# An S4D layer and a mixture of experts on one core: decay powers in pairs, the last block transposed in SBUF, a new order for the front

## The chip, the cores and the metric

The kernel runs on one core of one Trainium2 chip. The metric is device time in microseconds (us) of one execution. Three executions of the kernel before took 728.3 to 729.1 us, with a median of 728.49.

## What is computed

One sequence of 2048 tokens with 512 channels passes through two residual layers.

```python
def A(u):                                  # S4D: a long convolution per channel
    A_ = -exp(log_A_real) + 1j * A_imag    # (512, 128), dt = exp(log_dt)
    C  = (C_real + 1j * C_imag) * dt
    K  = 2 * einsum("dn,dnl->dl", C, exp(A_ * dt * pos)).real    # 512 kernels of length 2048
    return causal_convolution(u, K) + u * D_skip

def B(x):                                  # mixture of 8 experts, one for each token
    gates = softmax(x @ wg)                # wg: 512 x 8
    h = gelu(einsum("nd,edf->nef", x, w1)) # w1: 8 x 512 x 1792
    y = einsum("nef,efd->ned", h, w2)      # w2: 8 x 1792 x 512
    return y of the token's best expert    # its weight, normalised over one choice, is 1

h   = u + A(layernorm(u))
out = h + B(layernorm(h))
```

## The kernel before

**How the order is set.** The kernel is written as some two thousand tasks. `at(engine, cost, function, arguments, r=reads, w=writes)` records one with what it reads and writes, and the table `ORD` gives each its place in the program by name and ordinal; nothing is planned from the costs while it is built. Tasks that can run on two engines carry "AV", and `ON` says for each whether it runs on ScalarE (ACT) or VectorE (DVE). The table `FILL` says after which tasks TensorE (PE) runs how many filler matmuls on zeros (L952 in the profile), keyed by a task's name and ordinal. Each engine takes its own instructions strictly in this order. Transfers are issued by SyncE's queue (SP), and those whose rows are looked up by GpSimd (POOL).

**The front, up to about 363 us.** The 512 channels are four blocks of 128. For each block, `tables` makes powers of the decay and of the rotation and multiplies them out to the convolution kernel:
- `t_e` (L612): exp(l * alp) for l = 0..63, one ACTIVATE of 128x128 for each power; `t_ep` (L572) six more for the steps of 32; `t_r6`, `t_f6` (L579, L584) round six multiples of the angle phi and subtract.
- `t_wi`, `t_wr` (L661, L663, L668) on DVE multiply powers and angles for a quarter of the block; `t_kg` (L675) is PE's sum over the 128 states, 64 small matmuls into one PSUM bank, which the trace counts as 128; `t_kt` (L679) copies the bank to SBUF and `t_d` (L683) adds D_skip to its first column.

`conv` then runs on blocks, with eight pieces (rc) each: `c_load` and `c_s2` (L544) bring the kernel into the form of short matrices, `c_z` (L735) multiplies by them on DVE, `c_ia` (L742, L743) is 16 matmuls back, and `c_ys` (L748) copies their bank to SBUF. The result has time and channel in the wrong places, so `c_yst` (L751) stores each piece to `yd_scratch` in DRAM and `c_y1` (L774) loads four quarters (q) of the block back with the axes exchanged. `c_ib` (L779) transforms each quarter (two matmuls, which the trace counts as four), `c_add` (L782) adds the residual x, and the quarter goes on to routing: `r_s4` (row statistics, L994), `r_tr` and `r_ev` (transpose by PE and copy, L999, L1003), `r_lg` (logits, L1011), and `r_hd`, the store of its rows to `hd_scratch`.

**Between the layers.** `r_st` (L990) takes statistics of the first two blocks' columns, loaded again by `r_ld`; `r_ag` (L1040) joins them; `r_sd` and `r_rs` give 1/std; `r_le` copies logits, `r_lt` transposes them, `r_a` (L1079 to L1083) picks the expert. `r_vs` (L1103) stores mean, 1/std and token number of each row in 16 bytes behind the row's 512 columns. Counts and prefix sums give each expert its list of rows (`r_B`, `r_t0`, `r_i0`, L1187).

**The experts, from about 363 us.** For each expert, `m_ga` (L1292) gathers its rows from `hd_scratch` by POOL, `m_ln` normalises (L1334), and the two matrix products run in three passes, with each operand split in a high and a low part (L1380 on ACT, L1384 on DVE; L1393 to L1395 and L1416 to L1418 or L1425 to L1427 on PE). `m_ot` (L1442) scales and adds the residual, and `m_sc` (L1285) scatters rows to the output.

## Time and profile before

| what | value |
|---|---|
| median of three executions | 728.49 us |
| the profiled execution, its own time | 730.45 us |
| span of that execution in the trace | 728.6 us |
| mean granted clock of PE | 0.968 of full speed |
| last instruction of the tables (`t_wr` of block 3) ends | 297.9 us |
| last `c_ys` (block 3) starts | 333.41 us |
| first gather of rows starts | 363.62 us |
| last scatter starts | 722.11 us |

The trace covers one execution. Its span begins at the first and ends at the last instruction, and the execution's own time is 1.85 us longer. In the lines below, "L661" is a line of the program, "out<-in" names the tiles, "x32" counts instructions, and after the bar stand busy time in us and the mean of one in ns.

### The profile page before, as it was taken

To read this page: it belongs to the slowest core of one execution; us is meant where nothing else is said; L and a number is where in the kernel's file an instruction comes from. 1 tells how busy PE (TensorE), PEld (TensorE's weight loads), DVE (VectorE), ACT (ScalarE), POOL (GpSimd) and SP (SyncE) were. 2 spreads that over 40 slices of the span, in tenths; PEclk is the share of its full clock that TensorE was granted. 3 is DMA by queue.
4 is the path that set the end of the run, shared out by engine and by line. 5 is a ranking of instruction groups with operands and counts; after the bars stand their busy time and mean duration, and the time that the engine had idled before them with its cause. 6 is when DMAs were issued, how large, how long until landed. Compare 5 with 4: busy or idle time off the path is not lost.

```text
span 728.6 us, 19922 instructions
## 1 busy us (share of the span) xinstructions
PE 657.8 (90%) x8184; PEld 577.3 (79%) x8184; DVE 565.4 (78%) x1063; ACT 455.8 (63%) x907; POOL 73.1 (10%) x65
## 2 busy tenths in 40 slices
PE   3688999988989998798779999999999999999995
PEld 2446898778777886585369999999999989898884
DVE  6999998899999998575768975666766777666752
ACT  6899999959965976111435545555555556566651
POOL 0000000000000000000015131040210302132201
PEclk9689999999999999999769999999999999999998
DMA  9994134657575696898757566456565667676620
GB/s 188 174 233 60 62 119 175 237 214 212 155 229 176 188 279 219 238 298 231 178 198 207 157 203 187 147 190 197 173 207 169 204 203 236 196 234 197 198 90 26
DMA packets 139256, 136.38 MB, mean 187 GB/s; under 512 B 42172, under 2 KB 108352, under 8 KB 138907
## 3 DMA queue, kind: packets, MB, share of 16 engines
q1 hardware_dynamic: 135674, 126.48, 60.2%
q0 software_dynamic: 3488, 8.60, 3.4%
q8 instruction: 65, 1.06, 0.6%
q14 instruction: 29, 0.23, 0.1%
HBM read 109.83 MB, written 29.52 MB: 191 GB/s over the span
## 4 chain that ended last, share of the span: by engine, by line
PE 46%; issue 18%; DVE 16%; DMA 10%; ACT 4%; SPq 2%; POOL 2%; POOLq 1%; DVEq 0%; ACTq 0%
DMA y<-yd_scratch 5%; PE ps_s L1393 4%; PE ps_s L1394 4%; PE ps_s L1395 4%; PE ps_kk L544 3%; PE pk L675 3%; PE ps_ga L742 3%; PE ps_pl L952 3%; PE ps_ga L743 3%; DMA yd_scratch<-ys 2%; PE ps_kk L1425 2%; SPq L389 2%; PE ps_s L779 2%; PE ps_kk L1427 2%; PE ps_kk L1426 2%
## 5 line engine op out<-in xcount | busy, mean ns | idle before, releaser
L1384 DVE TENSOR_TENSOR l<-r,h 128x1024 fp32r<-128x1024 f32 x112 | 136.5, 1223 | 53.0 <-ACT h L1380 50.3
L1380 ACT CAST h<-r 128x1024 fp32r<-128x1024 f32 x112 | 117.6, 1050 | 80.7 <-PE ps_s L1395 41.4
L1393 PE MATMUL ps_s<-xh,h 128*128 128x288 f32 (+5 forms) x448 | 129.8, 290 | 0.0
L1395 PE MATMUL ps_s<-xl,h 128*128 128x288 f32 (+5 forms) x448 | 128.1, 286 | 0.0
L1394 PE MATMUL ps_s<-xh,l 128*128 128x288 f32 (+5 forms) x448 | 127.9, 286 | 0.0
L1393 PEld LDWEIGHTS ps_s<-xh,h 128*128 128x128 f32 x448 | 85.5, 191 | 3.1 <-issue 0.5
L1394 PEld LDWEIGHTS ps_s<-xh,l 128*128 128x128 f32 x448 | 85.4, 191 | 2.5 <-issue 0.5
L1395 PEld LDWEIGHTS ps_s<-xl,h 128*128 128x128 f32 x448 | 85.3, 190 | 0.0
L1398 ACT ACTIVATE g<-ps_s 128x288 f32<-128x288 f32 (+5 forms) x112 | 43.3, 387 | 65.4 <-PE ps_s L1395 50.3
L1405 DVE TENSOR_TENSOR gl<-g,gh 128x288 fp32r<-128x288 f32 (+5 forms) x112 | 46.6, 426 | 20.3 <-ACT gh L1401 18.0
L952 PE MATMUL ps_pl<-ident 128*128 128x512 f32 (+1 forms) x156 | 53.9, 492 | 0.0
L612 ACT ACTIVATE e<-alp 128x128 f32<-128x128 f32 x256 | 53.2, 309 | 0.0
L742 PE MATMUL ps_ga<-u,mi 128*128 128x128 f32 x256 | 50.9, 280 | 2.4 <-issue 2.4
L743 PE MATMUL ps_ga<-u,mi 128*128 128x128 f32 x256 | 49.9, 276 | 2.5 <-issue 2.5
L1285 POOL DMA_INDIRECT out_dram<-ot,si x20 | 24.4, 1218 | 222.8 <-DVE ot L1442 219.4
L952 PEld LDWEIGHTS ps_pl<-ident 128*128 128x128 f32 x156 | 28.1, 216 | 21.2 <-issue 20.3
L735 DVE TENSOR_TENSOR u<-ps_kk,u 128x1024 f32<-128x1024 f32 x32 | 38.5, 1217 | 7.7 <-PE ps_kk L544 7.7
L742 PEld LDWEIGHTS ps_ga<-u,mi 128*128 128x128 f32 x256 | 38.8, 191 | 6.6 <-issue 5.4
L743 PEld LDWEIGHTS ps_ga<-u,mi 128*128 128x128 f32 x256 | 38.9, 192 | 2.9 <-issue 2.9
L675 PE MATMUL pk<-e,vr 128*32 128x64 f32 x1024 | 36.2, 230 | 3.4 <-issue 2.0
L675 PEld LDWEIGHTS pk<-e,vr 128*32 128x32 f32 x1024 | 33.5, 144 | 5.3 <-issue 3.5
L675 PE MATMUL pk<-wi,vi 128*32 128x64 f32 x1024 | 36.1, 228 | 1.4 <-issue 0.8
(288 smaller groups left out, 1582.4 us busy)
## 6 DMA issues: line engine op xcount, KB each, us to landing
r<-in_B_w_dram SPq DMA_DIRECT2D x112, 512.0 KB
u<-ud_scratch SPq DMA_DIRECT2D x32, 512.0 KB
ud_scratch<-xn SPq DMA_DIRECT2D x16, 512.0 KB
yd_scratch<-ys SPq DMA_DIRECT2D x32, 256.0 KB
y<-yd_scratch SPq DMA_DIRECT2D x16, 512.0 KB
xu<-in_A_u_dram SPq DMA_DIRECT2D x16, 256.0 KB
xd_scratch<-in_A_u_dram SPq DMA_DIRECT2D x8, 512.0 KB
xr<-xd_scratch SPq DMA_DIRECT2D x6, 512.0 KB
```

The source lines that it names most:

```text
L612: A.activation(tb[blk, "e"][:, l // 2, :, l % 2], par(alp, blk), AF.Exp, scale=float(l))
L675: T.matmul(pk[32 * g:32 * g + 32, 64 * j:64 * j + 64], v[:, :, 8 * g + j], w[:, :, 8 * g + j, :], start=n == 0, stop=n == 1, skip_group_ch ...
L742: T.matmul(pa[:, c], mi[:, 4 * rc + rr, 64:192], z[:, 0, c], start=True, stop=False)
L743: T.matmul(pa[:, c], mi[:, 4 * rc + rr, 0:128], z[:, 1, c], start=False, stop=True)
L952: T.matmul(p[:, 0:128 * k], w, _view(ident, [[0, k], [1, 128]]), start=first, stop=True, skip_group_check=True)
L1380: A.copy(tile_(("h" + n, e, f), list(r.shape), F32R, pool="wp", name="h" + n, bufs=2), r)
L1384: V.tensor_tensor(tile_(("l" + n, e, f), list(r.shape), F32R, pool="wp", name="l" + n, bufs=2), r, t_["h" + n, e, f].bitcast(F32), op=OP.s ...
L1393: T.matmul(o[:, 0:CAPS[e]], a, xh, start=c == 0, stop=False)
L1394: T.matmul(o[:, 0:CAPS[e]], b, xh, start=False, stop=False)
L1395: T.matmul(o[:, 0:CAPS[e]], a, xl, start=False, stop=c == 3)
L1398: A.activation(tile_(("g", e, f), [128, CAP], name="g", bufs=2)[:, 0:CAPS[e]], t_["pf", e, f][:, 0:CAPS[e]], AF.Gelu_apprx_tanh)
L1405: V.tensor_tensor(tile_(("gl", e, f), [128, CAP], F32R, name="gl", bufs=3)[:, 0:n], t_["g", e, f][:, 0:n], t_["gh", e, f][:, 0:n].bitcast( ...
```

## The change

1. **Decay powers in pairs.** alp and phi get a second copy beside them that holds twice the value (`p_tw`, two DVE instructions). One ACTIVATE over both makes the powers l and 2l of 128x2x128 elements. `t_e` is now 42 ACTIVATEs for each block, 21 pairs and 21 single ones; `t_ep` is three, `t_r6` and `t_f6` four each. Power 0 is a memset on GpSimd (`t_e0`, `t_e1`).
2. **D_skip by PE.** `t_d` is gone; a matmul of the identity with `dpad` opens the bank of `t_kg`.
3. **Block 3 without the trip to DRAM.** All 32 rows of block 3 stay in `ys3`. Four VectorE transposes by 32x32 blocks (`c_yt`) exchange the axes into `yt3`, and eight pairs of matmuls (`c_ic`) over half the columns each take the place of the four `c_ib`.
4. **Statistics with the last rows.** The last 128 columns lie in `hx` with mean, 1/std and token number behind them, so that the store of block 3's rows (`r_hd`, now issued by ACT's queue) carries all; `r_vs` is gone. `r_ld` and `r_st` work in eight halves, `r_rs` in four.
5. **End of the last expert.** The last six matmuls of each of its two chunks stand together by chunk.
6. **Order.** `ORD` has new places for the whole front and `ON` new engines for some copies; `FILL` is unchanged. Two of block 2's four `c_y1` are issued by ACT, and two use the ring of the u1 tiles.

```diff
     'p_pol': [15],
...
-    'c_ys': 'AVAAAAVAVAAAAVVAAAAAAAAAVVVAAAAA',
+    'c_ys': 'VAAVAAVAAAAAAAAAAAAAAAAAVAAAVVAA',
...
+    def p_tw(k):
+        t = (alp2, phi2)[k]
+        V.tensor_scalar(t[:, 1, :], t[:, 0, :], 2.0, None, op0=OP.mult)
...
+    def pair(t, blk, two):
+        return t[:, 0:1 + two, 128 * blk:128 * blk + 128]
...
-        for k in range(6):
-            A.activation(ep[:, k, :], par(alp, blk), AF.Exp, scale=float(32 << k if k else 0))
+        for k, n, two in ((1, 64, 1), (3, 256, 1), (5, 1024, 0)):
+            A.activation(ep[:, k:k + 1 + two, :], pair(alp2, blk, two), AF.Exp, scale=float(n))
...
-        for l in range(l0, l0 + n):
-            A.activation(tb[blk, "e"][:, l // 2, :, l % 2], par(alp, blk), AF.Exp, scale=float(l))
+    HEAD = [l for l in range(1, 64) if (l & -l) in (1, 4, 16)]
+    POWERS = [l for l in HEAD if l < 32] + [l for l in HEAD if l > 32]
+
+    def t_e0(blk):
+        nc.gpsimd.memset(mk(blk, "e", [128, 32, 128, 2])[:, 0, :, 0], 1.0)
+
+    def t_e(blk, i):
+        for l in POWERS[3 * i:3 * i + 3]:
+            a, b = (256 * (k // 2) + k % 2 for k in (l, 2 * l))
+            two = l < 32
+            A.activation(_view(tb[blk, "e"], [[b - a, 1 + two], [2, 128]], a), pair(alp2, blk, two), AF.Exp, scale=float(l))
...
+        T.matmul(_view(pk, [[64, 8]]), ident, dpad[:, 32 * blk + 8 * jc:32 * blk + 8 * jc + 8], start=True, stop=False, skip_group_check=True)
...
-    def t_d(blk, jc):
-        k0 = tb[blk, ("kt", jc)][:, :, 0]
-        V.tensor_tensor(k0, k0, dpad[:, 32 * blk + 8 * jc:32 * blk + 8 * jc + 8], op=OP.add)
...
+    def c_yt(j):
+        if ("yt", j // 2) not in cv:
+            cv["yt", j // 2] = env["wp"].tile([128, 32, 64], F32, name="yt3", tag="w2", bufs=2)
+        V.transpose(_view(cv["yt", j // 2], [[1, 32], [64, 32]], 32 * (j % 2)), _view(env["ys3"], [[1, 32], [128, 32]], 32 * j))
...
+        t = cv["y1", blk, q] = utile(False) if blk == 2 and q % 2 else mp.tile([128, 2, 512], F32, name="y1")
+        (nc.scalar if blk == 2 and q in (0, 3) else nc.sync).dma_start(t, _dram(yd, [[32 * 128, 128], [16 * 128, 2], [1, 512]], (blk * 32 * 128 + 4 * q) * 128))
...
+    def c_ic(c, q):
+        if ("po", 3, q) not in cv:
+            cv["po", 3, q] = psp.tile([128, 512], F32, name="ps_" + ("s1", "kk")[q // 2], tag=("s1", "kk")[q // 2], bufs=2)
+        for h in range(2):
+            T.matmul(_view(cv["po", 3, q][64 * h:64 * h + 64], [[128, 4], [1, 64]], 64 * c), ibc[:, 64:128],
+                     cv["yt", c][:, 16 * h + 4 * q:16 * h + 4 * q + 4, :], start=True, stop=True)
...
+        env["hx"] = hp.tile([128, 16, 132], F32, name="hx")
...
-        nc.sync.dma_start(_dram(hd, [[16 * HW, 128], [HW, 4], [1, 128]], 4 * b4 * HW + 128 * blk), hs[blk, b4])
+        last = blk == 3
+        (nc.scalar if last else nc.sync).dma_start(_dram(hd, [[16 * HW, 128], [HW, 4], [1, 128 + 4 * last]], 4 * b4 * HW + 128 * blk),
+                                                   env["hx"][:, 4 * b4:4 * b4 + 4, :] if last else hs[blk, b4])
...
-    def r_vs():
-        nc.sync.dma_start(_dram(hd, [[16 * HW, 128], [HW, 16], [1, 4]], 512), t_["val"])
...
+    def ends(e, f):
+        return e == E - 1 and f > 11 and by_token(e)
...
-            for k in chunks(e):
+            for f, k in [(n, f - 12) for n in (12, 13)] if ends(e, f) else [(f, k) for k in chunks(e)]:
```

What the new order does shows best at two places. The first is PE's program just ahead of and behind the last `c_ia` of block 3 (L742, L743 before; L759, L760 now). In the kernel before, the last two of these 16 matmuls are followed by block 2's first `c_ib` (L779), fillers, routing transposes and the other three:

```order
L742 MATMUL ps_ga<-u_4274,mi 128x128
L743 MATMUL ps_ga<-u_4274,mi 128x128
L779 MATMUL ps_s_4509<-y_4355,ibc 64x512 x2
L952 MATMUL ps_pl<-ident,zero 128x128 x3
L999 MATMUL ps_ga<-ident,xr 128x128 x8
L1011 MATMUL ps_pl<-ys,wgp 32x128 x4
L999 MATMUL ps_ga<-ident,xr 128x128 x4
L1011 MATMUL ps_pl<-ys,wgp 32x128 x8
L779 MATMUL ps_s_4563<-y_4515,ibc 64x512 x2
```

In the changed kernel two `c_ib` of block 2 (L794; one reads a y tile, one a u1 tile) stand ahead of the last `c_s2` (L550, four of its matmuls) and the last `c_ia`:

```order
L759 MATMUL ps_ga<-u_4224,mi 128x128
L760 MATMUL ps_ga<-u_4224,mi 128x128
L794 MATMUL ps_s_4353<-y_4341,ibc 64x512 x2
L794 MATMUL ps_s_4366<-u_4363,ibc 64x512 x2
L550 MATMUL ps_kk<-ks,m_84 128x128 x4
L759 MATMUL ps_ga<-u_4261,mi 128x128
L760 MATMUL ps_ga<-u_4261,mi 128x128
```

So the two transforms moved from behind block 3's last back transform to ahead of it. The second place is DVE's program at the end of the front, where "xr" and "h" are the residual tiles of blocks 2 and 3, and "st" the statistics. Before, each addition waits for a quarter's transform:

```order
L782 TENSOR_TENSOR xr<-xr,ps_s_4509 128x512
L994 BN_STATS st<-xr 128x6 x4
L1003 COPY ys<-ps_ga 128x512 x2
L782 TENSOR_TENSOR xr<-xr,ps_s_4563 128x512
L994 BN_STATS st<-xr 128x6 x4
L782 TENSOR_TENSOR h_4265<-h_4265,ps_s_4580 128x512
L994 BN_STATS st<-h_4265 128x6 x4
L782 TENSOR_TENSOR h_4265<-h_4265,ps_s_4589 128x512
L1040 BN_AGGR r_val<-st 128x2 x4
```

Now the four transposes (L769) stand between block 2's last addition and block 3's, whose residual tile is "hx":

```order
L804 TENSOR_TENSOR xr<-xr,ps_s_4366 128x512
L1022 BN_STATS st<-xr 128x6 x8
L769 STREAM_TRANSPOSE yt_4439<-ys_4013 128x32x32 x2
L769 STREAM_TRANSPOSE yt_4451<-ys_4013 128x32x32 x2
L1018 BN_STATS st<-hr 128x6 x2
L1088 CAST r_cb<-r_rt 128x264
L804 TENSOR_TENSOR hx<-hx,ps_s_4457 128x4x128
L804 TENSOR_TENSOR hx<-hx,ps_s_4462 128x4x128
L1022 BN_STATS st<-hx 128x6 x4
L804 TENSOR_TENSOR hx<-hx,ps_kk 128x4x128
```

Two of block 2's additions and their statistics moved to ahead of the last `c_ys`, and the transposes stand where DVE waited for loads.

More of the change, by code (lines that the diff above doesn't have):

```diff
@@ new lines @@
+    'p_ev': [18, 20, 79],
+    'p_tw': [19, 23],
+    'p_at': [21],
+    't_e0': [22, 201, 391, 559],
+    't_e1': [24, 152, 383, 508],
+    't_r': [25, 188, 372, 542],
+    't_r6': [28, 85, 287, 555],
+    't_e': [29, 67, 36, 33, 59, 46, 64, 51, 57, 40, 69, 42, 45, 32, 228, 214, 244, 224, 241, 254, 248, 249, 218, 203, 262, 211, 231, 206,
+        414, 422, 410, 432, 399, 398, 400, 417, 402, 424, 421, 401, 413, 420, 611, 580, 607, 565, 617, 590, 570, 566, 595, 561, 585, 574,
+        594, 583],
@@ new lines @@
+    'p_th': [30],
+    'l_s1': [31],
+    'u_stats': [60, 34, 49, 80],
+    't_f': [35, 41, 48, 52, 55, 58, 196, 215, 220, 225, 243, 256, 376, 378, 389, 405, 418, 427, 546, 549, 552, 560, 576, 581],
+    'x_cp': [43, 50, 235, 158, 111, 198, 68, 39],
+    't_ep': [44, 191, 384, 544],
+    't_f6': [47, 129, 331, 569],
+    't_vf': [54, 56, 61, 62, 73, 177, 179, 187, 189, 195, 374, 377, 385, 388, 437, 597, 598, 601, 606, 620],
+    'u_mean': [63, 83],
+    'u_dev': [65, 89],
+    't_tb': [66, 115, 131, 154, 268, 308, 326, 358, 433, 461, 486, 524, 614, 653, 679, 708],
@@ L347, in s4d @@
     cp = st.enter_context(tc.tile_pool(name="s4c", bufs=1))
-    phi = cp.tile([128, 512], F32, name="phi")
-    alp = cp.tile([128, 512], F32, name="alp")
     amp = cp.tile([128, 512], F32, name="amp")
@@ L368, in s4d @@
     ta = tsa.enter_context(tc.tile_pool(name="s4tab2", bufs=1, side="right", reuse_waits="tile"))
+    phi2, alp2 = (ta.tile([128, 2, 512], F32, name=n) for n in ("phi", "alp"))
+    phi, alp = phi2[:, 0, :], alp2[:, 0, :]
     at = plan.add
-    ldt = cp.tile([128, 4], F32, name="ldt")
-    dt4 = cp.tile([128, 4, 4], F32, name="dt4")
-    dtw = cp.tile([128, 4, 4], F32, name="dtw")
+    ldt = fp.tile([128, 4], F32, name="ldt")
+    dt4 = fp.tile([128, 4, 4], F32, name="dt4")
+    dtw = fp.tile([128, 4, 4], F32, name="dtw")
     stt6 = fp.tile([128, 64, 6], F32, name="stt6")
@@ L804, in conv @@
             at("AV", EV, c_ys, blk, rc, r=["pa" + j] + ["h3/0/o"] * last, w=[y])
-            at("S", 0.87, c_yst, blk, rc, r=[y], w=[f"yd{n}/{rc}"])
-        ys = [f"{('yh', 'yk')[q // 2] if last else 'y1'}/{4 * blk + q}" for q in range(4)]
+            if not last:
+                at("S", 0.87, c_yst, blk, rc, r=[y], w=[f"yd{n}/{rc}"])
+        ys = ["yt" if last else f"{'ub' if blk == 2 and q % 2 else 'y1'}/{4 * blk + q}" for q in range(4)]
         for q in range(4):
@@ L816, in conv @@
             if last:
[L817 to L818 removed]
+                j = f"{('po', 'pv')[q // 2]}/{12 + q}"
+                for c in range(2):
+                    at("T", 0.55, c_ic, c, q, r=[f"yt/{c}", "ibc/0"], w=[f"{j}/{c}"])
+                at("V", 0.66, c_add, 3, q, r=[j, "hq/0", "hq/1"], w=[f"h3/0/{q}"])
                 route(blk, q, [f"h3/0/{q}"])
@@ L1314, in m_wu @@
     def m_wu():
-        V.memset(sm("wui", [PR, 1], I32), 0)
-        gather(sm("wur", [PR, 128]), t_["wui"], cst["id"])
+        V.memset(eid[:, 0:1], 0)
+        gather(sm("wur", [PR, 128]), eid[0:PR, 0:1], cst["id"])
     def m_ga(e, k):
```

421 lines of the change are left out of this document (204 added, 217 removed), and 91 rows, old and new, of tables (ORD, RINGS).

## The prediction

> **What bounds the kernel now.** I read the page first, then busy time by stage, then the chain of work that ended last.
>
> ```profile
> span 728.6 us, 19922 instructions
> PE 657.8 (90%) x8184; PEld 577.3 (79%) x8184; DVE 565.4 (78%) x1063; ACT 455.8 (63%) x907; POOL 73.1 (10%) x65
> ```
>
> PE is busy 90% of the span, but that is an average, and in the front it includes fillers that serve no result. The windows by stage say more. Their columns are the stretch, its length, busy us of PE, weight loads, DVE, ACT and POOL, the granted PE clock, the DMA share and GB/s.
>
> ```profile
> 57.00:298.00 241.00, 218.47 (x4937) 187.79 (x4935) 226.80 (x300) 197.37 (x422) 0.00 (x0) 1.00 0.56 178
> 65.00:328.00 263.00, 236.25 (x5109) 204.87 (x5110) 237.85 (x331) 194.24 (x421) 1.13 (x1) 1.00 0.62 194
> 328.00:363.00 35.00, 26.74 (x207) 15.57 (x206) 22.56 (x83) 10.60 (x19) 0.00 (x0) 0.88 0.76 205
> ```
>
> From 57 to 298 us DVE is busy 226.8 of 241 us: it paces the tables. From 328 to 363 us no engine is full, so the chain there is latency. What DVE waits for in the first stretch, in its view of waits (total us, times, longest):
>
> ```profile
> DVE wi L661 <- ACT ks L530: 2.0, 1, 2.0
> ...
> DVE wi L661 <- ACT s L579: 0.8, 1, 0.8
> ```
>
> Only 2.8 us of its 14.2 us idle is put down to ACT. The chain (start, us, what) then gives the hand-over to the experts:
>
> ```profile
> 298.81 1.08 PE ps_s L779 x4
> 299.89 2.26 PE pk L675 x107
> ...
> 316.25 0.89 PE ps_kk L544 x8
> 317.14 0.22 PE ps_ga L742 x2
> ...
> 333.41 0.59 ACT ys L748
> 334.02 2.49 DMA yd_scratch<-ys
> ...
> 337.22 8.30 DMA y<-yd_scratch
> ...
> 357.20 6.41 DMA r<-in_B_w_dram
> 363.62 5.75 DMA rows<-hd_scratch,r_gi
> ```
>
> After the last `c_ys` at 333.41, which I call E, 12.1 us pass in a store and a load until block 3's y is there (337.22 + 8.30), and 30.2 until the first gather at 363.62. From there the experts run, PE bound: nothing in them changes but the last 12 matmuls and some early placements, so what the gather gains, the end gains.
>
> **The tables.** Their last DVE instruction ends at 297.9; the groups of DVE (count, then busy us and mean ns) and of ACT:
>
> ```profile
> L530 DVE COPY ks<-ps_s 128x512 f32<-128x512 f32 x14 | 9.4, 685 | 3.9 <-PE ps_s L525 3.9
> L514 DVE TENSOR_SCALAR xn<-xu,mr 128x128 f32<-128x128 f32 x28 | 7.6, 430 | 0.0
> L584 DVE SCALAR_TENSOR_TENSOR s<-phi,s 128x128 f32<-128x128 f32 x24 | 5.2, 281 | 0.0
> L683 DVE TENSOR_TENSOR kt<-kt,dpad 128x8 f32<-128x8 f32 x16 | 2.7, 168 | 0.0
> L663 DVE TENSOR_TENSOR wi<-e,rf 128x1024 f32<-128x1024 f32 x16 | 19.5, 1219 | 0.0
> L445 DVE RECIPROCAL cw<-cw 128x512 f32<-128x512 f32 x1 | 3.4, 3353 | 0.0
> ...
> L612 ACT ACTIVATE e<-alp 128x128 f32<-128x128 f32 x256 | 53.2, 309 | 0.0
> L468 ACT COPY phi<-ps_s 128x512 f32<-128x512 f32 x1 | 0.6, 568 | 0.0
> ...
> 274.92 0.16 DVE L683 TENSOR_TENSOR kt<-kt,dpad 128x8 f32<-128x8 f32 x1
> 274.99 0.28 DVE L634 TENSOR_TENSOR vi<-amp,ep 128x128 f32<-128x128 f32 x1
> ...
> 296.67 1.22 DVE L668 TENSOR_TENSOR e<-e,af 128x1024 f32<-128x1024 f32 x1
> ```
>
> On DVE up to that instruction: six fewer copies of a PSUM bank (counted from `ON` and the order) at 0.67 (9.4/14), -4.0. Fifteen `t_d`: the next instruction starts 0.07 behind one, so I take 0.08 each, -1.2; the bound by the group's 0.168 is -2.5. `t_f6` goes from six to four each block; a pair should lie between 0.22 (5.2/24) and 0.69, I take 0.36, so 6 x 0.22 - 2 x 0.22 - 2 x 0.36 = 0.15 a block, -0.6. Four more `u_norm` instructions at 0.27, +1.1. `p_tw` is two of 512 elements, between 0.3 and 0.69 each, +0.8. The sum is **-3.9**.
>
> On ACT, 64 exponentials of 0.21 a block (53.2/256) become 21 of 256 elements and 21 of 128. The 512-element copy takes 0.57, so between the two 256 elements cost about 0.33, and a block saves 13.3 - 21 x 0.33 - 21 x 0.21 = 2.0, or 8 us in all; `t_ep` and `t_r6` save some 2.6 more, by the same prices, and six copies come in at 0.57, +3.4, less four norms of 0.2 or more. ACT is thus relieved of about 8 us, but it is not what DVE waits for: I price it at **0**, with -2.8 as the bound of the two rows above, and what a better order might do to the rest of DVE's idle time as a rival. The first exponential of a block now waits for a POOL memset, which waits for PE to be done with the block before. POOL is idle there (0.00 in the first window), and ACT has PSUM copies of 0.57 beside it; if that cover fails, four memsets of 128 elements a row that are as slow per element as L445, +3.4 at most. The identity matmul of `t_kg` is 16 small ones among 2048, **0**.
>
> **From the last table to E.** After it `t_kg` (2.26) and then block 3's pieces follow on PE with little room: 298 to 333 is a row of matmuls. Now two `c_ib` of block 2 stand ahead of the last two `c_ia`. Each is 1.08 (row 298.81), so +2.2. These two wait for their loads of y; PE cannot pass them, and the last `c_s2`, `c_ia` and so everything behind wait for it. Both loads are issued by ACT, in its order behind a `c_ys`, and one needs the y tile that the `c_ib` before it leaves. A load like it took between 5.0 us in block 2 and 8.3 in block 3:
>
> ```profile
> 293.65 5.02 DMA y<-yd_scratch
> ```
>
> In between PE has two `c_s2` (rows of eight matmuls in the chain, 0.89) and two `c_ia` (16 matmuls of 0.11, 1.8), 5.4 us. The wait is 0 for a load of 5.02 and 2.9 for one of 8.30, and could occur at both. I take +1.0, near the load of its own block, with 0 to 5.8 as ends. From the tables to E: **+3.2**, and E itself moves by -3.9 + 3.2 = -0.7.
>
> **From E to the gather.** DVE in the kernel before (start, us, in the bracket the idle time ahead):
>
> ```profile
> 350.09 0.51 DVE L1040 BATCH_NORM_AGGREGATE r_val<-st 128x2 f32<-128x18 f32 x4
> 350.52 0.81 DVE L994 BATCH_NORM_STATS2 st<-h 128x6 f32<-128x128 f32 x4
> 351.24 0.67 DVE L782 TENSOR_TENSOR h<-h,ps_s 128x512 f32<-128x512 f32 x1
> 351.83 0.51 DVE L1040 BATCH_NORM_AGGREGATE r_val<-st 128x2 f32<-128x18 f32 x4
> 354.77 0.29 DVE L1017 COPY r_ls<-ps_pl 128x128 f32<-128x128 f32 x1 [1.08 <-PE ps_pl L1011]
> 362.31 0.15 DVE L1187 TENSOR_REDUCE r_gi<-ps_kg 128x3 int32<-128x6 f32 x1
> ```
>
> Now `c_ys` takes 0.6 behind E, DVE has block 2's last addition and statistics to finish (0.35 more), and the four transposes start at E + 0.95. **No transpose is in the trace.** Each handles 1024 elements a row, as L663 does in 1.22 (1.13 from start to start). Ends: 0.7, were it twice as fast as that row per element less its fixed part, and 6.7, were it as slow per element as L445 (3.35 for 512). I take 1.13, the row with its size: E + 5.45. [...]
>
> Behind them DVE's work stands nearly without a gap. From the last addition's start to `r_gi`'s end it took 362.46 - 351.24 = 11.2 us, of which 1.1 idle (row 354.77) and 0.5 `r_ls` copies, which go to ACT, fall away: 9.6. New in front or in between are three additions (0.59 each from start to start, 1.8), three groups of statistics (0.72, 2.2), two of aggregates (0.43, 0.9), eight `r_st` of 0.18 with the cast and PE's step to the first addition (2.4): 7.3. So `r_gi` ends at E + 5.45 + 16.9 = E + 22.35, and the gather starts at E + 22.6 if it waits for nothing else. It waits too for the last store of rows. That is now issued by ACT when DVE has the last 1/std, about 5 us ahead of `r_gi`; the store in the chain took 2.49, so it lands at about E + 21, 1.6 us to spare. In the kernel before, `r_gi` ended at 362.46 and the gather started at 363.62, so something else, by the order the 16-byte store `r_vs`, held it; that is gone. From E to the gather 30.2 become 22.8: **-7.4**.
>
> **The end.** PE's matmuls stand 0.23 apart:
>
> ```profile
> 717.14 0.39 PE L1416 MATMUL ps_kk<-h,gh 128*128 128x512 f32 x1
> 717.37 0.39 PE L1417 MATMUL ps_kk<-l,gh 128*128 128x512 f32 x1
> ...
> 719.42 1.13 DVE L1442 SCALAR_TENSOR_TENSOR ot<-ps_kk,cwt,rows 128x128 f32<-128x128 f32 x4 [2.23 <-PE ps_kk L1418]
> ...
> 722.11 0.96 POOL L1285 DMA_INDIRECT out_dram<-ot,si  x1 [0.30 <-issue]
> ```
>
> The first chunk is done three matmuls earlier, so its scaling and scatter come 0.7 earlier; the second scatter then waits for the second chunk's scaling (done at 721.58) and not for POOL: **-0.6**.
>
> **Sum.** -3.9 + 3.2 - 7.4 - 0.6 = -8.7. The profiled execution of 730.45 (span 728.6 and 1.85 around it) becomes 721.75; it lies 1.96 above the median, so the forecast is 728.49 - 8.7 = **719.8**.
>
> **Rivals.**
> - *Loads hold PE ahead of E.* Both `c_ib` wait 2.9 us: +4.8 on the forecast, 724.6. For it speaks the one load of 8.30, against it those of block 2. Chance 0.17.
> - *DVE's idle time shrinks with ACT's load.* If half the 14.2 us goes: 712.7. Against it speaks that only 2.8 is put down to ACT; for it, that the rest is waits on PE banks which ACT's copies also free. 0.14.
> - *Slower: the fillers no longer fall in PE's gaps.* `FILL` is keyed by task and ordinal, and those tasks have moved. From 65 to 328 us the granted clock is 1.00. Where PE idled it fell:
>
> ```profile
> 365.70:369.10 3.40, 0.01 (x1) 0.00 (x0) 0.00 (x0) 1.04 (x1) 1.03 (x2) 0.91 1.02 394
> 369.10:372.50 3.40, 2.03 (x9) 1.66 (x10) 2.37 (x5) 0.43 (x1) 0.00 (x0) 0.50 0.03 12
> ```
>
> A gap of 3.4 us put the next stretch to half clock. Each us of PE work at half clock takes twice as long; with PE on the path, 17.4 us of span at half clock eat the gain of 8.7, and 30 us (a fall in each of the four blocks, each over twice the 3.4 of the second row) give 719.8 + 15 = 734.8. [...] Chance 0.12.
> - *The change doesn't do what it says:* a transpose costs 3.35, L445's time, not 1.13: +8.9, 728.7, no change. 0.07.
>
> **How the numbers follow.** The forecast (716.5 to 723 by the ends of its small terms) has 0.50. A measurement of this kernel can tell about 0.2% from no change, that is 727.0 to 729.9. Faster: 0.50 + 0.17 + 0.14, less a margin for sums of mishaps, 0.80; same 0.08; slower 0.12. The range of 712.0 to 728.5 takes in all but the slower rival, half the last one, and the far end of the second.
>
> **What would show it.** Right: `t_wr` of block 3 ends near 294, no ACT wait on DVE, the transposes take 1.1 each, gather 22 to 23 us behind the last `c_ys`, the clock at 1.00 up to 328. Wrong: PE idle on y ahead of the last `c_ia` for over 3 us; transposes over 2 us; a clock below 1.00 there; the gather released by a store.

## The result, and the profile after

The changed kernel takes 738.59 us (median of four executions, 736.65 to 740.25), the kernel before, beside it, 728.39 (726.67 to 729.10). The ratio is 1.0143, with a 95% interval of 1.0105 to 1.0180: the change makes the kernel 1.4% slower. The forecast of 719.8 and its range were missed on the other side. The profiled execution of the changed kernel took 736.95 us. In what follows medians are over all executions of a run, and ratios leave out single executions that were slow (the slowest: one of 2233 us in `f1_half_fill` and one of 1876 us in `f4_half_weights_loads`).

The page, as before (span, then busy us, share and count by engine):

```profile
span 735.0 us, 19910 instructions
PE 657.4 (89%) x8244; PEld 583.2 (79%) x8244; DVE 567.5 (77%) x1042; ACT 457.1 (62%) x806; POOL 76.1 (10%) x73
```

The sums hardly differ, so the time went into waits and into where the work stands. The span is therefore cut at the same four events in both traces (te: end of the last `t_wr`; E: end of the last `c_ia`; start of the first gather; end of the span):

| stretch | before, us | after, us | forecast | measured |
|---|---|---|---|---|
| start to te | 297.9 | 300.8 | -3.9 | +2.9 |
| te to E | 35.4 | 41.5 | +3.2 | +6.1 |
| E to gather | 30.3 | 32.2 | -7.4 | +1.9 |
| gather to end | 365.0 | 360.5 | -0.6 | -4.5 |
| span | 728.6 | 735.0 | -8.7 | +6.4 |

Of the last -4.5, 2.0 only give back the row above: the rows, gathered later, landed in 3.67 us (5.75 before), so that the first expert matmul starts 40.7 us behind E before and 40.6 after. The other 2.5 are more than the forecast's 0.6; a second profile of the unchanged kernel (`b0_before_again`, below) already differs from the first by 1.2 there, and the rest was not taken apart. The windows of the changed kernel (columns as in the prediction), for the whole tables and then for the prediction's three stretches:

```profile
0.00:300.80 300.80, 253.05 (x5066) 211.24 (x5066) 273.41 (x447) 243.99 (x448) 1.84 (x12) 0.97 0.67 176
57.00:298.00 241.00, 219.38 (x4949) 191.37 (x4948) 221.43 (x280) 196.22 (x340) 1.29 (x6) 0.99 0.56 171
65.00:328.00 263.00, 237.47 (x5174) 209.42 (x5168) 227.68 (x284) 191.97 (x337) 2.42 (x7) 0.97 0.59 181
328.00:363.00 35.00, 28.42 (x262) 19.89 (x260) 30.84 (x91) 11.66 (x22) 0.00 (x0) 0.98 0.59 155
```

The same sum over the tables of the kernel before:

```profile
0.00:297.90 297.90, 254.60 (x5036) 208.38 (x5036) 276.66 (x471) 245.80 (x556) 0.20 (x4) 0.97 0.67 182
```

DVE's work fell by 3.25 us, close to the forecast, and yet te is not earlier: DVE idles 27.4 us in place of 21.2. In the second profile of the unchanged kernel te is 300.6 and DVE idles 24.1 us. So the +2.9 in the table is not told from spread; what both profiles show is that the 3 us of work that DVE was spared became idle time. Its waits up to te, the largest of the changed kernel (total us, times, longest):

```profile
DVE xn L560 <- PE ps_kk L550: 5.7, 5, 3.9
DVE u L752 <- PE ps_kk L550: 3.8, 3, 2.1
DVE vi L653 <- PE pk L695: 3.3, 1, 3.3
```

All name PE. In the kernel before the largest two were these, 3.1 and 2.6:

```profile
DVE u L735 <- PE ps_kk L544: 3.1, 4, 1.8
DVE xn L554 <- PE ps_kk L544: 2.6, 5, 1.0
```

The chain that ended last, behind te (start, us, what), shows the rest of the story:

```profile
297.76 2.21 PE ps_pl L980 x18
...
303.93 3.44 issue
307.37 1.98 PE ps_s L531 x45
309.34 1.58 PE ps_pl L980 x6
...
314.04 1.57 PE ps_pl L980 x6
...
330.36 6.10 DMA u<-yd_scratch
...
342.37 0.59 ACT ys L764
...
344.88 5.62 DVE yt L769 x3
...
365.10 8.38 DMA hd_scratch<-hx
...
374.53 0.97 POOL rows L1322
...
375.80 3.67 DMA rows<-hd_scratch,r_gi
```

Three things stand there that the prediction did not have on the path: fillers (L980, 18 and twice 6), PE standing for 3.44 us ("issue": it waits for nothing that the profile shows), and a store of rows that takes 8.38 us, as long as the load of y (8.30) that the change took away. The trip of block 3 through DRAM is indeed gone.

### The profile page after: what moved, and what is told of

It is laid out like the page before. It is cut to its first block, busy times and chain, and to the rows that moved or that the text cites. A ratio compares the mean times of both kernels' runs of the same rounds, so it can differ in the third digit from the quotient of the medians.

```text
span 735.0 us, 19910 instructions
## 1 busy us (share of the span) xinstructions
PE 657.4 (89%) x8244; PEld 583.2 (79%) x8244; DVE 567.5 (77%) x1042; ACT 457.1 (62%) x806; POOL 76.1 (10%) x73
## 4 chain that ended last, share of the span: by engine, by line
PE 51%; issue 18%; DVE 16%; ACT 8%; DMA 3%; POOL 2%; POOLq 1%; SPq 0%; DVEq 0%; ACTq 0%
PE ps_kk L550 5%; PE ps_s L1433 5%; PE ps_s L1434 5%; PE ps_s L1435 5%; ACT e L631 4%; PE pk L695 4%; PE ps_pl L980 4%; PE ps_s L531 3%; PE ps_ga L759 2%; PE ps_ga L760 2%; PE ps_kk L1466 2%; PE ps_ga L1466 2%; PE ps_kk L1467 2%; PE ps_kk L1468 2%; PE ps_ga L1468 2%
## 5 line engine op out<-in xcount | busy, mean ns | idle before, releaser
L1425 DVE TENSOR_TENSOR l<-r,h 128x1024 fp32r<-128x1024 f32 x56 | 68.6, 1224 | 30.2 <-ACT h L1421 30.0
L1421 ACT CAST h<-r 128x1024 fp32r<-128x1024 f32 x56 | 58.7, 1048 | 44.6 <-PE ps_s L1435 44.4
L1425 DVE TENSOR_TENSOR w<-r,w 128x1024 fp32r<-128x1024 f32 x56 | 68.5, 1224 | 20.8 <-ACT w L1421 19.8
L1421 ACT CAST w<-r 128x1024 fp32r<-128x1024 f32 x56 | 58.8, 1049 | 28.1 <-PE ps_ga L1468 16.6
L631 ACT ACTIVATE e<-alp 128x256 f32<-128x256 f32 (+1 forms) x168 | 54.3, 375 | 2.2
L759 PE MATMUL ps_ga<-u,mi 128*128 128x128 f32 x256 | 51.2, 282 | 3.8 <-DVE u L752 2.9
L980 PE MATMUL ps_pl<-ident 128*128 128x512 f32 (+1 forms) x156 | 50.1, 465 | 0.0
L760 PE MATMUL ps_ga<-u,mi 128*128 128x128 f32 x256 | 49.5, 275 | 0.0
L759 PEld LDWEIGHTS ps_ga<-u,mi 128*128 128x128 f32 x256 | 38.8, 191 | 8.5 <-DVE u L752 3.5
L980 PEld LDWEIGHTS ps_pl<-ident 128*128 128x128 f32 x156 | 26.4, 203 | 19.2 <-issue 18.5
L760 PEld LDWEIGHTS ps_ga<-u,mi 128*128 128x128 f32 x256 | 38.9, 192 | 0.0
```

The source lines that it names most:

```text
L631: A.activation(_view(tb[blk, "e"], [[b - a, 1 + two], [2, 128]], a), pair(alp2, blk, two), AF.Exp, scale=float(l))
L759: T.matmul(pa[:, c], mi[:, 4 * rc + rr, 64:192], z[:, 0, c], start=True, stop=False)
L760: T.matmul(pa[:, c], mi[:, 4 * rc + rr, 0:128], z[:, 1, c], start=False, stop=True)
L980: T.matmul(p[:, 0:128 * k], w, _view(ident, [[0, k], [1, 128]]), start=first, stop=True, skip_group_check=True)
L1421: A.copy(halves(e, f, n, 0), r)
L1425: V.tensor_tensor(halves(e, f, n, 1), r, t_["h" + n, e, f].bitcast(F32), op=OP.subtract)
```

## The experiments

Theories: (F) fillers stand on the path in the new order; (W) weight loads and the last row stores collide; (P) PE's pauses, above all the one at 303.9 with half clock behind it, come from the loads around them; (D) pairs or the new order of the tables lose time themselves. All ratios are against the kernel before on the same chip. Single executions of one kernel spread by up to 1% either way in these sessions, so intervals are wide, and a difference of 1 to 3 us between two profiled executions is not told from that spread: a second profile of the unchanged kernel has te at 300.6 (297.9 in the first).

**Each suspect by itself.** `e1_sp_store`: the last rows' stores on SP's queue, as before.

```diff
-        (nc.scalar if last else nc.sync).dma_start(_dram(hd, [[16 * HW, 128], [HW, 4], [1, 128 + 4 * last]], 4 * b4 * HW + 128 * blk),
+        nc.sync.dma_start(_dram(hd, [[16 * HW, 128], [HW, 4], [1, 128 + 4 * last]], 4 * b4 * HW + 128 * blk),
```

> The changed kernel, with block 3's row stores issued by SyncE's queue again, where they stand ahead of the second expert weights, in place of ScalarE's queue. In the changed kernel the last row store was issued at 365.10 us and landed 8.38 us later, and the gather started 32.2 us behind the last c_ys. Theory A: four weight loads went ahead of the rows because the rows left SyncE's queue; expected is a landing about 3 us after the issue, a gather 25 us behind the last c_ys, and a time 4 to 7 us shorter. Rival B: the store is slow by its own shape (runs of 528 bytes), so it still takes 8 us and the time stays within 1 us. Rival C: the gather comes some 7 us earlier, but the experts then wait for the delayed weights and the time stays within 2 us.

Measured: 736.77, ratio 1.0120 [1.0085, 1.0155]. The gather came at E + 28.6 in place of 32.2, and its rows then took 5.31 us to land in place of 3.67; the first expert matmul starts at E + 38.8 (40.6). Some 1.8 us, a part of W.

`e2_copies_early`: two copies of the input in DRAM (`x_cp`), which lie beside PE's pauses, placed elsewhere.

```diff
-    'x_cp': [43, 50, 235, 158, 111, 198, 68, 39],
+    'x_cp': [43, 50, 159, 158, 111, 158.5, 68, 39],
```

> The changed kernel, with the two copies of the input to xd_scratch that stood behind block-wide stores of u (issued at 90.4 and 95.9 us) moved ahead of them, to about 47 us, as in the kernel before. Theory A: the copies fill the DMA engines (share 1.06 to 1.19 from 93 to 100 us), PE pauses 2.63 us at 98.5 for that reason and then runs at half clock up to 107; without them pause and half clock go, the last table instruction of block 1 ends 3 to 5 us earlier than 171.3, and the time is 2 to 4 us shorter. Rival B: the tables there are paced by ScalarE, whose exponentials take 11% of the chain; then nothing moves by more than 1 us.

Measured: 736.52, 1.0093 [1.0056, 1.0130]. The pause of PE at 98.5 fell from 2.63 to 1.27 us and te stayed (302.2). Nothing won that the interval can tell. (The same pause was 1.54 us in `e6_weights_first`, below, which left these copies in place.)

`e3_singles`: every power an ACTIVATE of its own, all else as changed.

```diff
-            A.activation(_view(tb[blk, "e"], [[b - a, 1 + two], [2, 128]], a), pair(alp2, blk, two), AF.Exp, scale=float(l))
+            for l2, o in ((l, a), (2 * l, b))[:1 + (l < 32)]:
+                A.activation(_view(tb[blk, "e"], [[2, 128]], o), par(alp, blk), AF.Exp, scale=float(l2))
```

> The changed kernel, with every pair of powers of t_e made by two ACTIVATEs of 128 elements at the same place (power 0 stays with GpSimd). By the price of the prediction (0.33 for a pair, 0.21 for a single one) ScalarE's busy time grows by 84 x 0.09 = 8 us, and the time by as much if ScalarE paces the tables. By the trace of the changed kernel (37.0 us for 84 pairs, 0.44 each, 0.227 for a single one) a pair costs what two single ones do: busy time and total time stay within 1.5 us.

Measured: 735.71, 1.0095 [1.0059, 1.0132]. Pairs neither cost nor save anything that can be told. The groups of the changed kernel and of the kernel before (count, busy us, mean ns) say why:

```profile
L631 ACT ACTIVATE e<-alp 128x256 f32<-128x256 f32 x84 | 37.0, 442 | 1.9
L631 ACT ACTIVATE e<-alp 128x128 f32<-128x128 f32 x84 | 19.1, 309 | 0.2
```

A pair takes 0.44 us (37.0/84), a single one 0.23 (19.1/84): 56.1 us for what took 53.2 in 256 singles.

**Undoing the order of the front.** `h1_old_order`: the old places for everything before the hand-over, new ones behind it, the old engines for the copies of the tables and `c_ys`, and one y tile less for block 2.

```diff
-    'l_x': [26, 5, 8, 37],
+    'l_x': [18, 5, 8, 36],
...
-    'p_tr': [15, 13, 53, 27],
+    'p_tr': [16, 13, 41, 63],
...
```

> The changed operations (pairs, D_skip by PE, block 3 transposed in SBUF, rows with their statistics, the end of the last expert), but with the order and the copies' engines of the kernel before for all tasks that stood ahead of the opening of the last block's tiles there; behind it the order of the changed kernel. The four loads of block 2's y use one tile, as before. Theory A: the new order cost the tables their time; then they end 3 to 4 us earlier than the 297.9 of the kernel before, and 5 to 7 earlier than the 300.7 of the changed one, and the total is at least 5 us below the changed kernel's. Rival B: the new operations cost it (pairs that save nothing on ScalarE, memsets and the identity matmul in new waits); then the tables end at 299 or later with the old order too.

Measured: 745.53, 1.0241 [1.0171, 1.0310]. te is 304.5; 3.4 of it is there already at the first `t_wr` (62.9, against 59.5), where ACT waits 4.9 us for DVE's doubled phi: `p_tw` stands too late there. The stores of rows took 9.85 us. Too much is changed at once to say what the new order costs.

`h2_no_pairs_old`: as `h1_old_order`, but powers and turns made singly as before, without `p_tw` and the memsets.

```diff
-        if k < 2:
-            at("V", 0.45, p_tw, k, r=[f"par/{k}"], w=[f"par/{k}"])
```

> As the run with the old order, but the powers are made one by one again by ScalarE (no doubled copies, no memsets by GpSimd); of the changes in the tables only the identity matmul in place of t_d is left. Theory P (the pairs cost the tables their time: doubled copies on DVE ahead of ScalarE's first powers, memsets that wait): the tables end at 296 to 298.5 us, some 7 us earlier than the 304.5 of the run with pairs. Rival I (the identity matmul, or the spread of executions): they end at 302 or later.

Measured, one execution: 742.94; first `t_wr` at 59.5 again, te 301.9. The 3.4 us at the first `t_wr` went with the pairs and `p_tw`.

`b0_before_again`: the kernel before, unchanged, for the spread of its trace.

> The kernel before once more, profiled: how far do the ends of its stages move from one execution to another? In the first profile the tables ended at 297.9 us, the last c_ia at 333.3 and the first gather started at 363.6. If all three come back within 1 us, the 300.1 to 304.5 us at which the tables ended in six of seven runs of the changed kernel's variants are a loss by the change; if they move by 3 us or more, that loss cannot be told from the spread.

Measured, one execution: 730.56, te 300.6, E 34.6 later, gather at E + 30.0. These two stages repeat within 0.8 us, the one from the gather to the end within 1.5 (363.6 against 365.0); te moves by 2.7. What repeats is DVE's busy time up to te, 276.48 (276.66).

`a1_no_pairs`: the changed kernel and its order, with the pairs, `p_tw` and the memsets taken out of it.

```diff
-        for k, n, two in ((1, 64, 1), (3, 256, 1), (5, 1024, 0)):
-            A.activation(ep[:, k:k + 1 + two, :], pair(alp2, blk, two), AF.Exp, scale=float(n))
+        for k in range(6):
+            A.activation(ep[:, k, :], par(alp, blk), AF.Exp, scale=float(32 << k if k else 0))
```

> The changed kernel in its own order, with all powers made one by one by ScalarE (no doubled copies, no memsets). Theory P: the tables end at 297 us or earlier in place of 300.8, and the time is 3 us or more shorter than the changed kernel's. Rival O (the new order's own waits: DVE waits for PE and for ScalarE's sines): the tables end at 300 to 304 as in the other runs, and the time stays within 2 us.

Measured: 736.78, 1.0109 [1.0057, 1.0162]. With `e3_singles` this closes D's first half: the pairs are no loss that these intervals can tell. Its second half, the new order of the tables by itself, stays open, since `h1_old_order` changed too much.

`h3_tail_only`: the tables of before with `t_d`, the changed kernel's tail, weights first (below), and two of block 2's `c_ib` behind the last `c_ia`. (Places behind the tables are 1000 higher in this kernel.)

```diff
-    'c_ib': [514, 482, 498, 536, 662, 642, 624, 699, 792, 726, 771, 800],
+    'c_ib': [520, 483, 501, 546, 672, 647, 633, 697, 1819.1, 748, 1771, 1819.2],
...
```

> The kernel before in its tables (powers one by one, t_d on DVE, old order up to the opening of the last block's tiles) with the changed tail: block 3 transposed in SBUF, statistics in the rows' store, the last expert's end; in it the first four weight loads stand ahead of the blocked loads of statistics columns, and block 2's two late transforms and their additions behind the last c_ia and the transposes. If the tail is worth what the run with the weights ahead showed (first expert matmul 36.8 us behind the last c_ia in place of 40.7, less up to 2.6 us for block 2's additions, which now follow the transposes), then with tables that end near 298 the time is 2 to 5 us below the kernel before: 724 to 727. If the transposes and the stores take back what the trip to DRAM cost, it is within 1 us of the kernel before.

Measured: 740.61, 1.0177 [1.0131, 1.0222]. te to E was 37.5, but `r_gi` ended at E + 30.9 (24.5 in the changed kernel): block 2's additions now stand behind the transposes, and DVE then waits 3.3 us for PE. This suggests that the two `c_ib` ahead of E, which the prediction charged with +3.2, are the cheaper place; the run differs in its tables too, so it does not show it.

**The loads around the pause.** `e5_late_loads`: two `c_load`, a `c_x` and a `c_y1` of the stretch later, on ACT's queue.

```diff
-        nc.sync.dma_start(u, _dram(ud, [[1024, 64], [0, 2], [1, 1024]], (blk * 8 + rc) * 128 * 512))
+        (nc.scalar if (blk, rc) in ((3, 0), (3, 6)) else nc.sync).dma_start(u, _dram(ud, [[1024, 64], [0, 2], [1, 1024]], (blk * 8 + rc) * 128 * 512))
...
```

> The changed kernel, with four loads that were issued between 302.98 and 304.57 us (two pieces of u for block 3, half of block 2's residual, a quarter of its y) issued by ScalarE's queue behind its copies of block 3's kernel, so some 5 to 10 us later. Theory A: the burst of loads behind the end of the tables (DMA share 0.98 from 304 to 311) holds up PE for 3.44 us at 303.9, where no engine's result is waited for, and the clock then stands at 0.50 up to 317; with fewer loads the pause falls below 2.2 us, the clock stays above 0.9, the stretch from the last table instruction to the last c_ys shrinks from 41.6 to 36 or 38 us, and the time by 3 to 5 us. Rival B: the pause is PE's own and has nothing to do with the loads; it stays at 3 us or more, and so does the half clock.

Measured: 736.56, 1.0108 [1.0063, 1.0153]. te to E fell from 41.5 to 37.7, the pause was 2.62 us (at 307.9), and the half clock behind it lasted 3.4 us in place of 10.2 (mean clock from 300 to 320 us 0.91 in place of 0.74). But the total is the same: te was 304.5 in that profile. Nor is the shorter half clock the loads' doing alone: `e6_weights_first`, below, leaves them in place, has a pause of 3.42 us at 303.6, and its matmuls run slow for 3.4 us behind it (306.97 to 310.34, the six fillers there at 1.58 us in all); the sixty of `c_s1` that follow take 1.24, against 1.90 in the changed kernel.

`e7_mi_later`: the loads of the back transform's matrices (`m_load`) at other places.

```diff
-    'm_load': [438, 357, 360, 332, 361, 320, 338, 341],
+    'm_load': [438, 371.4, 332, 371.1, 338, 371.3, 371.2, 320],
```

> The changed kernel, with five of the eight loads of the table mi issued behind block 0's first store of y (166 us) in place of 141 to 149 us. Theory A: PE's pauses of 2.54 us at 145.2 and 2.50 at 151.7 come from this burst (DMA share 0.98 to 1.03); they shrink to less than 2.5 in all, the last table instruction of block 1 ends 2 to 4 us earlier than 171.3, and the time is 2 to 3 us shorter. Rival B: the tables there are paced by DVE and ScalarE anyway, and the pauses are made up by 171: no change beyond 1 us.

Measured: 738.19, 1.0133 [1.0089, 1.0177]. The pauses near 145 and 151 us stay (2.34 and 2.48), so P is refuted for these two pauses and these loads.

**Weights first.** `e6_weights_first`: the first expert's four weight loads ahead of the loads of statistics columns (`r_ld`) in SP's queue.

```diff
-    'm_w1': [854, 906, 926,
+    'm_w1': [838.1, 838.2, 926,
...
-    'm_w2': [921, 917, 945,
+    'm_w2': [838.3, 838.4, 945,
...
```

> The changed kernel, with the first four loads of expert weights ahead of the two loads of statistics columns in SyncE's program that wait for a tile which DVE only frees behind its transposes (SyncE stood there from 340.7 to 351.5 us, and the weights came at 351.6 to 364, together with the stores of rows). Theory A: the gather waits for stores that share the DMA engines with these weights; with the weights loaded during the transposes (DMA share 0.00 to 0.09 there) the last row store lands within 4 us in place of 8.4, the gather starts 25 to 26 us behind the last c_ys in place of 32.2, and the time is 5 to 7 us shorter. Rival B: what the gather gains the experts give back, as in the run with the stores on SyncE's queue (3.7 gained, 2.4 given back): the time is 0 to 2 us shorter.

Measured: 734.71, 1.0105 [1.0043, 1.0167]; in its profile the gather comes at E + 28.5 (32.2) and the first expert matmul at E + 36.8 (40.6). SP's own timeline in the changed kernel (start, us, what; L1014 is `r_ld`, L1405 and L1409 are weights):

```profile
340.71 10.79 SPq L1014 DMA_DIRECT2D hr<-hd_scratch  x2
351.60 0.42 SPq L1405 DMA_DIRECT2D r<-in_B_w_dram  x1
...
358.90 1.20 SPq L1405 DMA_DIRECT2D r<-in_B_w_dram  x1
360.20 1.44 SPq L1409 DMA_DIRECT2D r<-in_B_w_dram  x2
```

and in this experiment:

```profile
338.89 0.97 SPq L1405 DMA_DIRECT2D r<-in_B_w_dram  x2
339.91 1.57 SPq L1409 DMA_DIRECT2D r<-in_B_w_dram  x2
348.86 5.20 SPq L1014 DMA_DIRECT2D hr<-hd_scratch  x2
```

SP stood 10.8 us at two loads whose tile `r_st` frees, and `r_st` now stands behind the four transposes on DVE. Everything behind them in SP's queue waited: windows of the changed kernel in that time and behind it (DMA share and GB/s are the last two columns),

```profile
343.00:351.00 8.00, 6.59 (x75) 4.23 (x74) 8.00 (x6) 2.25 (x4) 0.00 (x0) 1.00 0.02 8
351.00:364.00 13.00, 7.20 (x79) 3.78 (x74) 12.41 (x64) 6.32 (x14) 0.00 (x0) 0.90 0.80 187
364.00:374.00 10.00, 6.17 (x26) 3.79 (x26) 3.50 (x10) 0.00 (x0) 0.00 (x0) 0.62 0.92 286
```

and of the experiment:

```profile
341.00:349.00 8.00, 6.60 (x76) 4.12 (x76) 8.00 (x8) 2.25 (x4) 0.00 (x0) 1.00 0.78 271
```

The DMA engines idle for 8 us (share 0.02) and then carry the weights just when the rows must be stored. The issues of those stores, KB each and median us from issue to landing, changed kernel first:

```profile
hd_scratch<-hx ACTq DMA_DIRECT2D x4, 264.0 KB, 7.9
```

```profile
hd_scratch<-hx ACTq DMA_DIRECT2D x4, 264.0 KB, 4.4
```

That fits W, with 3.8 us up to the first matmul. By the ratios alone this run is not told from the changed kernel, since the intervals overlap; the pair `f1_half_fill` and `f3_half_weights` below differs by the same edit and is told apart.

`e8_three`: `e5_late_loads`, `e6_weights_first` and `e7_mi_later` together, with their three edits.

> The three edits of the other runs together (four loads late, weights ahead, mi later). If all three theories A hold, the changed kernel's 736 to 738 us become 722 to 727, faster than the kernel before; if only the weights matter, 730 to 732.

Measured: 732.11, 1.0056 [1.0021, 1.0090]. te to E 38.3, gather at E + 28.0. The gain of W comes through, and the kernel is still slower than before.

**The fillers.** `f1_half_fill`: half the fillers (rounded down) behind every task in `FILL` but those at the start of the front (`p_tr`, `u_mean`, `u_var`) and at the hand-over (`r_tr`, `m_tr`, `m_g1`).

```diff
-    ('t_kg', 0): 3, ('u_s1', 0): 5, ('r_sw', 0): 3, ('u_s2', 0): 3, ('u_s2', 5): 2, ('c_s1', 0): 17,
+    ('t_kg', 0): 1, ('u_s1', 0): 2, ('r_sw', 0): 1, ('u_s2', 0): 1, ('u_s2', 5): 1, ('c_s1', 0): 8,
...
```

> The changed kernel, with the numbers of fillers from the first t_kg to the last c_s2 halved (rounded down; 145 become 64); those at the start and in the routing stay. Theory F: DVE's work in the tables fell by 3.2 us as forecast (276.6 to 273.4), but its idle time behind PE grew by 4 to 8, since the fillers, whose numbers weren't changed, now stand on the chain (21 us of it between 57 and 343 us, 10.6 and 11.3 in the two profiles of the kernel before). With half of them the chain loses some 8 to 10 us of fillers, the tables end at 296 us or earlier in place of 300 to 304, and the time falls by 4 to 8 us. Rival K: without them PE's clock falls (below 0.95 between 57 and 300 us) and the time is the same or longer. Rival G: the fillers only fill time that PE would wait in anyway; the tables end at 300 or later at the same clock.

Measured: 731.03, 1.0009 [0.9978, 1.0041]. This one edit takes the loss away. Its one profile shows only part of that: the span is 731.8 us (735.0), te 298.4, te to E 39.9. `f2_no_fill`: none of those fillers.

```diff
-    ('t_kg', 0): 3, ('u_s1', 0): 5, ('r_sw', 0): 3, ('u_s2', 0): 3, ('u_s2', 5): 2, ('c_s1', 0): 17,
...
```

> As the run with half the fillers, with none from the first t_kg to the last c_s2. Theory F: a further 5 us or more if the clock holds; where it falls below 0.9 the gain is lost again, and the time lies between the run with half of them and the changed kernel. Rival G: no change.

Measured: 738.38, 1.0135 [1.0077, 1.0192]. And `b1_before_half`: the same halving in the kernel before.

> The kernel before, with the same fillers halved. Theory F: its fillers were placed for its own order, mostly in time that PE waited in; the time changes by less than half of what the changed kernel gains (0 to 3 us shorter, or longer by the clock). If it gains as much as the changed kernel does, the fillers don't explain the difference between the two.

Measured: 732.96, 1.0053 [1.0028, 1.0077]. The three belong together. Shares of the chain between 57 and 343 us, by line: the changed kernel, `f1_half_fill` and the kernel before (`ps_pl` is the fillers' bank; L980, L976 and L952 are the same line):

```profile
by line: PE ps_kk L550 12.8%; ACT e L631 11.1%; issue 10.2%; PE pk L695 10.0%; PE ps_pl L980 7.3%; PE ps_s L531 6.8%; PE ps_ga L759 6.0%; PE ps_ga L760 5.3%; DVE u L752 3.8%; PE ps_s L794 2.5%; DVE wi L680 2.2%; DMA u<-yd_scratch 2.1%; DVE 
```

```profile
by line: ACT e L627 12.0%; PE ps_kk L546 11.4%; issue 11.1%; PE pk L691 8.8%; PE ps_ga L755 6.3%; PE ps_ga L756 5.6%; PE ps_s L527 4.4%; DVE u L748 3.7%; DVE wi L676 3.1%; PE ps_s L790 2.5%; ACT ks L532 2.5%; DMA u<-yd_scratch 2.2%; DVE vi 
```

```profile
by line: DMA y<-yd_scratch 12.3%; PE ps_kk L544 8.6%; PE pk L675 8.1%; PE ps_ga L742 7.8%; issue 7.5%; PE ps_ga L743 7.4%; DMA yd_scratch<-ys 5.5%; PE ps_s L525 3.8%; PE ps_pl L952 3.7%; PE ps_s L779 3.3%; DVE vi L637 2.4%; DVE vs L630 2.2%
```

Fillers hold 7.3% of 286 us of the chain, 21 us, after the change, against 3.7%, 10.6 us, before; halved, they hold 2.4 us. The profiles agree on the place: te is 300.1 to 308.8 in the nine profiles of the new order with all fillers, and 296.3 to 299.4 in the four with half of them. But the chain alone does not price a filler: halving took 8.5 us of them off the chain of the kernel before as well (10.5 to 2.0), and that kernel got slower. In the kernel before, the same fillers do more good than harm (halving them costs 0.5%); in the changed one more harm than good. With none, the clock falls; here `f2_no_fill` over the tables:

```profile
57.00:300.00 243.00, 209.48 (x4822) 188.33 (x4822) 220.93 (x279) 195.64 (x339) 1.28 (x6) 0.90 0.56 170
```

A granted clock of 0.90 (0.99 in the changed kernel) goes with the loss of the whole gain. With half the fillers in both kernels, measured on one chip, the change is worth 0.3% (730.75 against 732.96, medians without the execution of 2233 us); the executions overlap (725.7 to 733.6 and 728.1 to 736.9), so this is hardly told from no change.

**The repairs together.** `f3_half_weights` is `f1_half_fill` with the edit of `e6_weights_first`; `f4_half_weights_loads` adds `e5_late_loads`; `f5_half_weights_again` repeats the first of the two in another session.

> Half the fillers and the first four weight loads ahead of the blocked loads of statistics columns. By theory F and the run with the weights ahead (first expert matmul 3.8 us earlier behind the last c_ia) the sum is 8 to 12 us below the changed kernel: 725 to 729, level with the kernel before or up to 4 us faster.

> Half the fillers, the weights ahead, and the four late loads of block 3 issued by ScalarE's queue. If the pause behind the tables (2.58 us at 301.8 with half the fillers and the weights ahead) shrinks further, 1 to 2 us below the run without the late loads, so 723 to 725; if the loads do nothing there, the same as it.

> Half the fillers and the weights ahead once more, in more rounds, to narrow its interval (0.9928 to 0.9991 of the kernel before): by the first result 0.996, about 726 us beside 729; if that was chance, 1.000 or more.

Measured: 725.55, ratio 0.9960 [0.9928, 0.9991]; 726.16, 0.9929 [0.9901, 0.9956]; 726.12, 0.9952 [0.9917, 0.9988]. All three beat the kernel before, by 0.4 to 0.7%. On one chip, `f3_half_weights` (ten executions) is 3.8 us faster on average than `f1_half_fill` (nine), with a 95% interval of 1.2 to 6.5 worked out from the executions: that shows the gain of the weights' place. In `f4_half_weights_loads` PE's pause behind te is down to 0.53 us (2.58 in `f3_half_weights`), yet te to E is 37.4 (37.6) and the time that of `f5_half_weights_again` on the same chip: the late loads shorten the pause, and the total gains nothing that can be told. In the profile of `f3_half_weights` the gather starts at 361.70, E + 27.8.

## Why the prediction was wrong

**The tables: -3.9 was +2.9 (0.2 against the second profile of the kernel before).** The step that failed first is "From 57 to 298 us DVE is busy 226.8 of 241 us: it paces the tables". DVE's own terms were right in sum (-3.9 forecast, -3.25 measured). But the same row had PE busy for 218.5 us, the view of waits puts another 10.3 us of PE's idle time there to no releaser, and it puts 9.3 of DVE's own 14.2 us of idle time to PE: PE paced the tables as much as DVE did. In the new order DVE's freed time went into waiting for PE, which carries fillers between the matmuls that DVE needs. `FILL` is keyed by task, so the change moved the fillers without touching the table. The prediction named that as its slower rival, but priced it through the clock ("a fall in each of the four blocks") and not as work on the path; the clock over the tables was 0.99. That the fillers cost the new order time is shown by `f1_half_fill` and `b1_before_half`: from 1.0143 to 1.0009, 1.3% or about 9.8 us of the 18.8 by which the forecast was missed (some 6 to 13 by the two intervals), where the same edit made the kernel before 0.5% slower. Which of the moved tasks carries how much was not taken apart.

**ACT's load at 0: right by luck, since the relief itself was not there.** 0.33 for a pair was 0.44, and with the copies that moved to it ACT did 243.99 us of work up to te, where it had done 245.80.

**From the tables to E: +3.2 was +6.1.** The two `c_ib` cost 2.16 as forecast, the wait for y 0.36 in place of 1.0, so the first rival fell; the second fell too, since DVE's idle time grew. The other 3.6 come from PE. Windows of the changed kernel at the pause and behind it:

```profile
303.60:307.40 3.80, 0.36 (x9) 0.22 (x7) 0.00 (x0) 0.59 (x1) 0.00 (x0) 0.91 0.98 341
307.40:317.00 9.60, 8.86 (x146) 8.21 (x146) 1.38 (x2) 1.17 (x2) 0.00 (x0) 0.50 0.42 163
```

PE stood for 3.44 us, and its clock was then 0.50 for 9.6 us with 8.86 us of matmuls in them: 60 of `c_s1` took 1.90 us there (310.92), where 64 had taken 1.09 at a clock of 1.00 (296.67). The kernel before paused there as well, in two pieces of 2.17 and 1.63, and its clock stayed at 1.00. But in the trace of the changed kernel a pause of 2.63 us at 98.5 was followed by 3.4 us at 0.50, so a half clock came behind a shorter pause too. Behind a pause of 3.42 in `e6_weights_first` the matmuls ran slow for 3.4 us, behind the one of 3.44 in the changed kernel for 9.6. So the length of the pause did not settle how long the half clock lasted, nor, with it, the 3.6.

**From E to the gather: -7.4 was +1.9.** Two steps failed. "I take 1.13" for a transpose: DVE's timeline of the changed kernel has the four at 7.52 us, 1.88 each, so the term was 3.0 too small.

```profile
342.99 7.52 DVE L769 STREAM_TRANSPOSE yt<-ys 128x1024 f32<-128x1024 f32 x4 [0.17 <-ACT ys L764]
```

`r_gi` still ended at E + 24.5, 2.2 later than forecast, as the work behind the transposes was counted well. The larger error is "it lands at about E + 21, 1.6 us to spare": the store of rows was taken at 2.49 us, from a store to `yd_scratch`, and took 8.38, was issued 1.8 us ahead of `r_gi`'s end and not 5, landed at E + 31, and released the gather, one of the prediction's own signs of being wrong. With the weights ahead (`e6_weights_first`) the row stores still have a median of 4.4 us and the last lands at E + 27.4, so 2.49 was too small even without that collision. (By the prediction's own terms the landing was near E + 20, and its sum has 22.8 where the text has 22.6; both slips are small.) The prediction had asked what the transposes hold up on DVE, and not who waits for that: `r_st` behind them frees the tiles that SP's queue stands at, and the weights behind that in SP's queue then meet the stores. `e6_weights_first` and `f3_half_weights` show it: 3.8 us in the profile of the first, 0.4 to 0.5% by the ratios (1.0143 to 1.0105, 1.0009 to 0.9960).

**The end: -0.6 was right.** The second scatter starts 1.84 us behind the start of the last matmul (2.43 before). In the changed kernel:

```profile
726.66 0.40 PE L1458 MATMUL ps_ga<-w,gl 128*112 128x512 f32 x1
```

```profile
728.50 0.96 POOL L1315 DMA_INDIRECT out_dram<-ot,si  x1 [0.41 <-DVEq L1613]
```

**The account.** About 9.8 us fillers (6 to 13), 2.8 to 3.8 the weights' place, 3.0 transposes: some 16 of 18.8, by terms whose intervals are wide and which may share time. The pause's half clock (up to 3.6 in the profile of the changed kernel) may share time with the fillers, three of whose pieces stand around it in the chain; the runs that shortened it did not shorten the total by what can be told, so that part stays open.

## What to carry to other kernels

Work that is there only to keep a clock up is placed for one order: when tasks move, count how much of it stands on the chain of the new order (here 21 us, against 10.6 before) and halve it as a first experiment: here the kernel with half of it was 1.3% faster than with all of it, and with none of it that gain was lost at a clock of 0.90 over the tables (0.99 with all). Two engines that are each busy nine tenths of a stretch may pace it together (here PE for 218.5 and DVE for 226.8 of 241 us), and relief of one alone may be worth little: the 3.25 us taken off DVE became idle time. When a long step is put into an engine's queue, follow the first buffer that it keeps from coming free through the queue that waits for it, to what stands behind there (here 7.52 us of transposes on DVE, and 10.79 in which SP's queue stood at two loads with the weights behind them).
